# Windowed attention and a shrinking MLP on one core: the masks of the first three tiles move from TensorE to VectorE, in a new order

## The chip, the cores and the metric

The kernel runs on one core of a Trainium2 chip. The metric is the device time of one execution in microseconds (us). Each time shown is of one execution; the median of several is compared. The core has TensorE (PE, matrix products into the eight PSUM banks), VectorE (DVE), ScalarE (ACT), GpSimd (POOL) and SyncE (SP). POOL, SP and ACT issue DMAs, each into a queue of its own.

## The reference, cut to what matters

```python
scores = scale * np.matmul(q, k.transpose(0, 1, 3, 2))       # 4 batches, 8 heads, 768 positions, head size 64
keep = is_global | is_local                                   # first 8 keys, or the last 96 before the query
bias = -slopes[:, None, None] * dist[None, :, :]              # one slope a head, dist 96 for far global keys
a = softmax(np.where(keep, scores + bias, -1e9))
x = (a @ v).transpose(0, 2, 1, 3).reshape(3072, 512)
h = x @ w_in                                                  # 512 x 2048
out = (h - np.tanh(h)) @ w_out                                # 2048 x 512
```

The inputs and the output are float32; the kernel multiplies in bfloat16 and sums in float32.

## The kernel before, in words

The 3072 rows are 24 tiles (u = 0 to 23) of 128 queries. Tiles 0 to 3 are the first of each batch and have one block of keys, their own. All others have two: their own and the previous tile's, into whose buffer the batch's first 8 (global) keys and values are copied (K.u, V.u). All heads of a tile are worked on together.

The whole program is one list written out by hand, ORDER (lines 17 to 65). Each word is an action, and every engine runs its own words in the order in which they stand there, one behind the other; semaphores are set by what the actions read and write. HOMES (lines 66 to 104) says which buffer or PSUM bank each value lives in, so that an action also waits until the former holder has been read. The words, with the lines that the profile shows:

- lq.u, lk.u, lv.u load queries, keys, values. For u < 3 (HW, line 141) q and k come in float32 over ACT's and SP's queue (L294) and are cast into kq by cq.u, ck.u (a suffix /a is ScalarE, /d VectorE; L229 and L231). All other loads go over POOL's queue, which casts on the way (L294 for u of 3 and 4, L297 from there on). in.j (L300) and out.j (L303) load the weights, also on POOL.
- rel (POOL, L235) writes the distances; from it VectorE makes dist (L240 to L242), slopes (L265), first (L245 to L249), turn and ident, and writes the ones beside the values (ones, L271). zero is a tile of zeros. table is an action that issues no instruction; ScalarE's table load is shown with em's line (L280).
- T.u turns q and k: on TensorE for u < 7 (PE_T; L317, L321, L312), followed by two evictions Te.u.1 (keys) and Te.u.0 (queries); by a DMA transpose on SP's queue from u = 7 on (L333).
- bm.m (TensorE, L275) multiplies dist by the slopes, two 128x512 products, and em.m (ScalarE, L280) takes exp of that: mk.m, a multiplicative mask. There are three: 0 for the first tile of a batch, 1 for the own block, 2 for the previous block.
- S.n are the scores of one or several blocks (L352). E.u.o is exp of a block (ScalarE, L359), M.u.o its product with the mask (VectorE, L363). AV.u multiplies by the values (L378), R.u divides (VectorE, L386 and L387), X.u transposes the result (L398), Xe.u evicts it into xT; from u = 8 on a DMA transpose does both.
- m1.g.f is x @ w_in for a group of tiles (L420), th its tanh (ScalarE, L430), g the difference (VectorE, L436), m2.u.c.a one of four parts of the second product (L445), ev its eviction and st the store (L454).

The first three tiles (BIASED = 3, line 144) differ: B.u (lines 343 to 345) puts dist times slopes into the PSUM bank first and S.u adds the scores to it, so that exp gives the masked weights at once and there is no M.u.

```python
def a_B(u):
    for o in blocks(u):
        bias(("s", u, o), mask_of(u, o), False)
```

The first actions of each queue, as ORDER has them: SP lk.1 lk.0 lk.2; ACT lq.1 lq.0 lq.2 table em.1 em.0 cq.0; POOL rel lq.3 lk.3 lv.0 lq.4 lk.4 lv.1 lv.2 in.1 in.0 lv.3 in.2; VectorE zero ones.0 slopes dist turn first ident ones.1 cq.1 ck.1 ck.0 Te.1.0 Te.0.0 ck.2 Te.3.0 Te.2.0 R.0 R.1 M.3.0; TensorE bm.1 bm.0 B.1 T.1 B.0 T.0 S.1 T.3 B.2 S.0 T.2 S.3 AV.0 S.2 AV.1 X.0 T.4 X.1 AV.2 bm.2 m1.0.0 AV.3 X.2 m1.1.0 X.3 S.4.

Of the kernel before, what the change touches and what calls it, by code (L numbers as in the profile page):

```python
# [22 lines left out]
lq.6 m1.1.4 th.2.0 M.4.1 m1.2.2 th.1.4 g.2.0 m1.0.4 th.2.6 g.1.4 lv.5 th.2.2 T.5 g.2.6 m1.1.8 th.0.4 Te.5.0/d Te.5.1/a
g.0.4 m1.0.8 th.1.8 g.2.2 lq.10 S.5 th.0.8 g.1.8 m1.2.10 E.5.1 g.0.8 m1.2.8 K.5 th.2.10 M.5.1 m2.2.0.0 lv.6 E.5.0
g.2.10 m1.2.4 th.2.8 M.5.0 m2.1.0.0 g.2.8 th.2.4 m2.0.0.0 g.2.4 out.3 m2.2.0.1 lk.8 m2.2.0.2 m2.0.0.1 AV.4 lq.7
m1.1.12 V.4 lk.10 R.4 m1.2.14 th.1.12 lq.8 m1.0.12 g.1.12 th.2.14 lk.9 g.2.14 m1.2.12 th.0.12 lk.7 m2.1.0.1 g.0.12
th.2.12 lq.9 X.4 g.2.12 AV.5 Xe.4/a m2.1.0.2 R.5 T.6 V.5 lv.7 m2.0.0.2 Te.6.1/a Te.6.0/d lk.11 X.5 m2.2.0.3 Xe.5/a
m2.0.0.3 ev.2.0/a T.10 S.6 ev.0.0/a m1.3.10 T.8 E.6.1 K.6 m1.3.0 E.6.0 M.6.1 T.7 m1.3.2 th.3.10 M.6.0 m2.3.0.0 T.9
th.3.2 g.3.10 m1.3.4 th.3.0 g.3.2 m2.1.0.3 g.3.0 th.3.4 AV.6 g.3.4 ev.1.0/a m1.3.6 R.6 st.1.0 m1.3.12 lv.15 th.3.6 V.6
m2.3.0.1 g.3.6 lq.12 th.3.12 S.7 g.3.12 lv.8 m2.3.0.2 E.7.1 K.7 lv.17 m1.3.8 E.7.0 lk.13 M.7.1 X.6 m2.3.0.3 Xe.6/d  # L30
lv.10 th.3.8 M.7.0 S.8 ev.3.0/a st.0.0 g.3.8 AV.7 lv.9 E.8.1 m1.3.14 V.7 R.7 lq.11 E.8.0 m2.4.0.0 M.8.1 lq.18 X.7
th.3.14 m2.4.0.1 M.8.0 lk.12 Xe.7/a S.9 g.3.14 lq.13 AV.8 E.9.1 K.9 m2.4.0.2 lq.15 R.8 E.9.0 m1.4.6 lv.11 M.9.1 Xe.8
m2.4.0.3 M.9.0 th.4.6 lv.12 T.11 m1.4.8 g.4.6 ev.4.0/a S.10 T.12 th.4.8 AV.9 E.10.1 K.10 g.4.8 m1.4.0 T.13 R.9 E.10.0
m2.5.0.0 M.10.1 Xe.9 m1.4.4 th.4.0 V.9 M.10.0 m1.4.10 th.4.4 g.4.0 m2.5.0.1 th.4.10 g.4.4 AV.10 lq.14 g.4.10 m2.5.0.2
R.10 lv.16 m1.4.2 V.10 lv.13 Xe.10 S.11 th.4.2 lk.15 m2.5.0.3 g.4.2 E.11.0 lk.14 K.11 m1.4.12 K.12 ev.5.0/d E.11.1
st.4.0 m1.4.14 M.11.0 lk.17 th.4.12 M.11.1 m2.6.0.0 th.4.14 st.5.0 g.4.12 m2.6.0.1 E.12.0 g.4.14 AV.11 M.12.0 m2.7.0.0
R.11 m2.7.0.1 V.11 Xe.11 S.12 m2.7.0.2 T.15 E.12.1 m2.7.0.3 E.13.1 M.12.1 T.14 m2.6.0.2 ev.7.0/d E.13.0 AV.12 M.13.1
st.7.0 m2.6.0.3 lq.16 M.13.0 m1.5.7 R.12 ev.6.0/a lv.14 m1.5.6 th.5.7 V.12 Xe.12 lk.16 m1.5.1 g.5.7 th.5.6 lq.17 AV.13
g.5.6 th.5.1 lv.18 m1.5.3 R.13 lq.23 m1.5.0 th.5.3 g.5.1 Xe.13 lk.18 m1.5.11 g.5.3 th.5.0 m1.5.8 g.5.0 lq.19 th.5.11
S.13 g.5.11 lk.19 th.5.8 m1.5.4 g.5.8 E.14.0 T.16 K.14 m1.5.2 K.15 E.14.1 M.14.0 T.17 m1.5.9 th.5.4 M.14.1 m1.5.13  # L40
th.5.2 g.5.4 m1.5.14 E.15.0 g.5.2 m1.5.10 th.5.13 M.15.0 th.5.14 m1.5.5 g.5.13 T.18 th.5.10 g.5.14 m2.8.0.0 th.5.5
g.5.10 m1.5.15 th.5.9 g.5.5 AV.14 th.5.15 g.5.9 m2.8.0.1 T.19 V.14 R.14 m1.5.12 m2.8.0.2 g.5.15 Xe.14 th.5.12 S.14
g.5.12 m2.9.0.0 E.15.1 K.16 m2.8.0.3 E.16.0 M.15.1 m2.9.0.1 ev.8.0/d E.16.1 AV.15 M.16.0 st.8.0 m2.10.0.0 lv.19 R.15
m2.9.0.2 lk.23 V.15 Xe.15 M.16.1 S.15 lv.22 m2.9.0.3 E.17.1 K.17 lv.23 m2.10.0.1 ev.9.0/d E.18.0 st.6.0 m2.10.0.2
M.17.1 lq.22 E.17.0 M.18.0 m2.10.0.3 st.3.0 st.2.0 M.17.0 AV.16 lv.21 m2.11.0.0 V.16 T.23 R.16 lv.20 AV.17 m2.11.0.1
R.17 st.9.0 Xe.16 ev.10.0/a m2.11.0.2 lk.20 V.17 Xe.17 m1.6.0 st.10.0 lq.21 S.16 th.6.0 lq.20 m2.11.0.3 g.6.0 E.19.1
K.19 lk.21 m1.6.9 ev.11.0/d E.19.0 m1.6.6 M.19.1 th.6.9 M.19.0 m1.6.4 th.6.6 g.6.9 m1.6.3 E.18.1 lk.22 g.6.6 m1.6.15
th.6.4 M.18.1 th.6.3 AV.19 g.6.4 AV.18 th.6.15 g.6.3 m1.6.12 R.18 m1.6.2 th.6.12 V.19 Xe.18 m1.6.8 g.6.15 th.6.2 R.19
m1.6.7 th.6.8 g.6.12 Xe.19 m1.6.1 th.6.7 g.6.8 m1.6.11 th.6.1 T.20 g.6.7 m1.6.5 th.6.11 g.6.1 T.21 m1.6.10 g.6.11
th.6.5 g.6.2 m1.6.14 th.6.10 T.22 g.6.5 m1.7.12 th.6.14 g.6.10 m1.6.13 th.7.12 g.6.14 m1.7.1 g.7.12 th.6.13 m1.7.10  # L50
g.6.13 th.7.1 S.17 g.7.1 th.7.10 m2.13.0.0 g.7.10 E.21.0 K.21 m2.12.0.0 K.20 E.20.0 M.21.0 m2.13.0.1 E.20.1 M.20.0
m2.12.0.1 M.20.1 m2.13.0.2 AV.20 m1.7.14 V.20 R.20 m2.13.0.3 th.7.14 Xe.20 m1.7.9 g.7.14 ev.13.0/a m2.12.0.2 th.7.9
m2.12.0.3 g.7.9 S.18 ev.12.0/a m1.7.5 E.21.1 K.22 m2.14.0.0 E.22.0 M.21.1 m1.7.3 th.7.5 M.22.0 m1.7.2 th.7.3 g.7.5
m2.14.0.1 E.22.1 g.7.3 AV.21 th.7.2 M.22.1 m2.14.0.2 V.21 g.7.2 m2.14.0.3 R.21 m1.7.0 ev.14.0/a Xe.21 S.19 st.14.0
th.7.0 m1.7.13 E.23.0 g.7.0 AV.22 th.7.13 M.23.0 m2.19.0.0 E.23.1 R.22 m1.7.7 V.22 Xe.22 m1.7.4 M.23.1 th.7.7 g.7.13
m2.18.0.0 th.7.4 g.7.7 m2.17.0.0 g.7.4 AV.23 m1.7.6 R.23 m1.7.8 th.7.6 Xe.23 m1.7.11 g.7.6 th.7.8 m2.18.0.1 g.7.8
th.7.11 m2.19.0.1 g.7.11 m2.19.0.2 m2.15.0.0 m2.16.0.0 m1.7.15 m1.8.0 th.7.15 m2.15.0.1 g.7.15 th.8.0 m1.8.1 g.8.0
m2.19.0.3 th.8.1 m1.8.15 g.8.1 ev.19.0/a m1.8.6 st.19.0 th.8.15 st.12.0 m1.8.3 g.8.15 th.8.6 m1.8.9 g.8.6 th.8.3
m2.17.0.1 g.8.3 th.8.9 m1.8.7 g.8.9 m1.8.10 th.8.7 m1.8.4 g.8.7 th.8.10 m2.15.0.2 g.8.10 th.8.4 m1.8.2 g.8.4 m1.8.5
th.8.2 m2.15.0.3 g.8.2 th.8.5 m1.8.11 g.8.5 ev.15.0/a m2.16.0.1 th.8.11 m2.20.0.0 g.8.11 m2.17.0.2 m2.22.0.0 m2.17.0.3  # L60
m1.8.8 ev.17.0/a m2.22.0.1 st.17.0 th.8.8 st.11.0 m2.21.0.0 g.8.8 m2.22.0.2 m2.18.0.2 m2.18.0.3 m1.8.13 ev.18.0/a
m2.20.0.1 st.18.0 th.8.13 m2.16.0.2 g.8.13 m2.16.0.3 m1.8.14 ev.16.0/a m1.8.12 th.8.14 m2.21.0.1 g.8.14 th.8.12
# [4 lines left out]
mk.0:2,3 mk.1:0,1 mk.2:6,7 f32.0.k:3 kq.0:1 f32.0.q:2 f32.1.k:1 kq.1:0 f32.1.q:0 f32.2.k:5 kq.2:3 f32.2.q:4 v.0:0
v.1:1 kq.3:2 v.2:2 kq.4:4 v.3:3 v.4:4 kq.5:0 v.5:5 kq.6:1 v.6:6 kq.7:4 v.7:7 kq.8:3 v.8:9 kq.9:0 v.9:4 kq.10:2 v.10:11
kq.11:1 v.11:5 kq.12:2 v.12:6 kq.13:3 v.13:7 kq.14:1 v.14:9 kq.15:0 v.15:8 kq.16:3 v.16:0 kq.17:2 v.17:10 kq.18:4
v.18:4 kq.19:1 v.19:11 kq.20:2 v.20:7 kq.21:4 v.21:6 kq.22:3 v.22:5 kq.23:0 v.23:1 tr.0.0:1 tr.0.1:7 qk.0:1 s.0.0:2,3  # L70
p.0.0:1 av.0:2,3 x.0:0 xt.0:2 xT.0:0 tr.1.0:6 tr.1.1:0 qk.1:0 s.1.0:4,5 p.1.0:0 av.1:4,5 x.1:1 xt.1:1 xT.1:1 tr.2.0:4
# [517 lines left out]
```

## Time and profile before

| What | us |
|---|---|
| median of three runs | 215.25 |
| the three runs | 214.08, 216.29, 215.25 |
| the profiled execution | 215.35 |
| its span, from the first instruction to the last | 213.5 |
| TensorE busy | 204.6 |
| VectorE busy | 130.4 |
| ScalarE busy | 120.5 |
| POOL busy | 76.9 |

A line of the timeline or of a group names the engine, the line, the operation, the tile written and the tiles read, the shape, and how often (x); times are us from the start of the span. Where two rows of the timeline overlap on one engine, the engine has begun the next instruction before the last has drained, so the step from start to start is shorter than the duration. The chain of waits follows the program back from its last instruction, at each step to what released it. Busy times by stretch have, behind the stretch and its length, the busy time and the number of instructions of each engine, the granted clock of TensorE, the mean load of the DMA engines and GB/s.

### The profile page before, as it was taken

How to read it: one execution, taken by the hardware profiler on the slowest of the kernel's cores; microseconds unless marked ns; L12 is line 12 of the kernel's file. 1: busy time of each engine (PE TensorE's matmuls, PEld its weight loads, DVE VectorE, ACT ScalarE, POOL GpSimd, SP SyncE). 2: the span in 40 equal slices, each digit the busy share in tenths (PEclk: the TensorE clock that was granted, in tenths of full speed). 3: DMA queues.
4: the chain of work that ended last, by engine and by line, in shares of the span. 5: the costliest groups of instructions: out<-in, count | busy, mean ns of one | idle time of the engine just before them, and what ended most of it. 6: DMA issues, size and time to landing. Idle time of an engine off the chain costs nothing.

```text
span 213.5 us, 4492 instructions
## 1 busy us (share of the span) xinstructions
PE 204.6 (96%) x1796; PEld 117.2 (55%) x1796; DVE 130.4 (61%) x264; ACT 120.5 (56%) x179; POOL 76.9 (36%) x101
## 2 busy tenths in 40 slices
...
GB/s 164 243 177 189 208 198 175 179 157 194 128 177 150 141 154 216 181 151 137 175 53 166 195 206 150 147 3 25 0 78 25 25 3 98 0 0 98 52 116 228
DMA packets 100884, 27.55 MB, mean 129 GB/s; under 512 B 91840, under 2 KB 99264, under 8 KB 100864
## 3 DMA queue, kind: packets, MB, share of 16 engines
...
q1 hardware_dynamic: 28048, 8.13, 23.5%
...
## 4 chain that ended last, share of the span: by engine, by line
PE 68%; issue 12%; DMA 10%; POOL 6%; DVE 1%; ACT 0%; SPq 0%; POOLq 0%; DVEq 0%; ACTq 0%
PE ps L420 30%; PE ps L445 28%; DMA qk<-kq 4%; POOL kq L297 3%; PE ps L352 3%; DMA f<-in_k_dram 3%; PE ps L378 3%; DMA out_dram<-ot 3%; POOL vb L297 2%; PE ps L398 1%; PE ps L317 1%; POOL out_dram L454 1%; PE ps L321 1%; PE ps L275 1%; PE ps L312 0%
## 5 line engine op out<-in xcount | busy, mean ns | idle before, releaser
L445 PE MATMUL ps<-w_out_bf,g 128*128 128x512 bf16 (+2 forms) x400 | 91.2, 371 | 0.0
L420 PE MATMUL ps<-xT,w_in_bf 128*128 128x512 bf16 (+2 forms) x576 | 90.5, 308 | 0.5 <-ACT ot L229 0.5
L436 DVE TENSOR_TENSOR g<-ps,th 128x512 bf16<-128x512 f32 x96 | 65.0, 688 | 38.7 <-ACT th L430 37.5
L430 ACT ACTIVATE th<-ps 128x512 f32<-128x512 f32 x96 | 56.7, 599 | 45.6 <-PE ps L420 44.8
L420 PEld LDWEIGHTS <-w_in_bf 128*128 128x128 bf16 x576 | 50.2, 98 | 33.9 <-issue 0.8
L445 PEld LDWEIGHTS <-g 128*128 128x128 bf16 x400 | 37.0, 98 | 38.0 <-DVE g L436 0.5
L454 POOL DMA_DIRECT2D out_dram<-ot x21 | 12.0, 576 | 106.3 <-ACT ot L229 86.5
L359 ACT ACTIVATE pr<-ps 128x1024 bf16<-128x1024 f32 x44 | 43.0, 1023 | 9.8 <-PE ps L352 9.8
L363 DVE TENSOR_TENSOR pr<-pr,mk 128x1024 bf16<-128x1024 bf16 x41 | 27.6, 687 | 8.0 <-ACT pr L359 7.9
L229 ACT COPY ot<-ps 128x512 f32<-128x512 f32 (+2 forms) x20 | 11.3, 565 | 26.6 <-PE ps L445 19.2
L297 POOL DMA_DIRECT2D vb<-in_v_dram x24 | 21.7, 912 | 5.1 <-DMA w_out_bf<-in_moe_w_out_dram 2.6
L297 POOL DMA_DIRECT2D kq<-in_q_dram x19 | 17.1, 911 | 12.4 <-DMA qk<-kq 8.2
L297 POOL DMA_DIRECT2D kq<-in_k_dram x19 | 17.1, 903 | 1.2 <-PE ps L352 0.5
L387 DVE TENSOR_TENSOR x<-ps,rden 128x512 bf16<-128x512 f32 x24 | 16.6, 692 | 0.8
L378 PEld LDWEIGHTS <-pr 128*128 128x128 bf16 x352 | 13.5, 98 | 4.2 <-issue 0.2
L378 PE MATMUL ps<-vb,pr 128*128 128x65 bf16 x352 | 14.8, 194 | 0.0
L352 PEld LDWEIGHTS <-qk 64*128 64x128 bf16 x352 | 10.2, 96 | 7.0 <-issue 6.3
L352 PE MATMUL ps<-qk 64*128 64x128 bf16 x192 | 10.1, 229 | 0.0
L231 DVE COPY vb<-vb 8x512 bf16<-8x512 bf16 x16 | 5.7, 356 | 5.9 <-PE ps L378 5.9
L275 PE MATMUL ps<-slopes,dist 128*128 128x512 bf16 x12 | 5.4, 587 | 3.1 <-DVE dist L242 3.1
L352 PE MATMUL ps<-qk,qk 64*128 64x128 bf16 x160 | 7.8, 217 | 0.0
L386 DVE RECIPROCAL rden<-ps 128x8 f32<-128x8 f32 x24 | 4.8, 199 | 2.8 <-PE ps L378 2.6
...
## 6 DMA issues: line engine op xcount, KB each, us to landing
...
w_out_bf<-in_moe_w_out_dram POOLq DMA_DIRECT2D x4, 512.0 KB, 13.1
w_in_bf<-in_moe_w_in_dram POOLq DMA_DIRECT2D x3, 512.0 KB, 10.5
...
```

Of the source, the lines that this page charges most:

```text
L229: nc.scalar.copy(out=out, in_=in_)
L297: eng(e).dma_start(out=dst, in_=rows_of(src, u).rearrange("h p d -> p h d"))
L352: nc.tensor.matmul(bank(("s", u, o), hh)[:, p * P : (p + 1) * P], buf(("qk", back[u] if o else u))[r, 1, p, :], buf(("qk", u))[r, 0, p, :] ...
L359: nc.scalar.activation(d, banks(("s", u, o), 0, 1), AF.Exp, bias=0.0, scale=scale)
L363: nc.vector.tensor_tensor(out=t, in0=t, in1=mk[:, mask_of(u, o)], op=ALU.mult)
L378: nc.tensor.matmul(t[:, h // (H // 2), h % (H // 2), :], buf(("p", u, o))[:, slot(h), :], buf(("v", back[u] if o else u))[:, h, 0 : Dh + 1 ...
L387: nc.vector.tensor_tensor(out=buf(("x", u)).rearrange("q (a h) d -> q a h d", a=2), in0=t[:, :, :, 0:Dh], in1=rden.to_broadcast([P, 2, H / ...
L420: nc.tensor.matmul(t[:, (f - f0) * n : (f - f0 + 1) * n], w_in_bf[j][:, c, fo : fo + P], x[:, c, 0:n], start=(c == 0), stop=(c == CD - 1),)
L430: nc.scalar.activation(h_view(buf(("th", g, f0)), g, m), h_view(bank(("h", g, f0)), g, m), AF.Tanh, bias=0.0, scale=1.0)
L436: nc.vector.tensor_tensor(out=buf(("g", g))[:, f0 : f0 + m, 0:n], in0=h_view(bank(("h", g, f0)), g, m), in1=h_view(buf(("th", g, f0)), g, ...
L445: nc.tensor.matmul(bank(part)[:, 0 : c1 - c0], buf(("g", g))[:, f, t * P : (t + 1) * P], w_out_bf[f // FJ][:, f % FJ, c0:c1], start=(f == ...
L454: eng(e).dma_start(out=out[turn_of[u] * P : (turn_of[u] + 1) * P, c0:c1], in_=buf(("ot", u))[:, c0:c1])
```

## The change

BIASED goes from 3 to 0: B.0, B.1 and B.2 are gone, the scores of tiles 0 to 2 start their banks themselves, and M.0.0, M.1.0 and M.2.0 multiply the masks in. warm() takes a bank, and the word zero:7 puts one product of the zero tile with itself (128x512, result unused) into bank 7. ORDER and HOMES are written anew throughout; all other actions are the same. The core of the diff, with the start of both orders and the stretch of the new one that holds lv.12 to T.11's loads:

```diff
 ORDER = """
-lq.1 lk.1 zero rel ones.0 lq.0 lk.0 lq.3 slopes lq.2 lk.2 lk.3 dist table lv.0 turn bm.1 first ident lq.4 ones.1 bm.0
-em.1 lk.4 cq.1/d ck.1/d B.1 lv.1 em.0 T.1 lv.2 B.0 cq.0/a ck.0/d in.1 Te.1.0/d Te.1.1/a T.0 in.0 S.1 Te.0.1/a Te.0.0/d
-cq.2/a ck.2/d E.1.0 lv.3 T.3 B.2 in.2 Te.3.1/a Te.3.0/d S.0 lk.5 T.2 E.0.0 lq.5 S.3 Te.2.0/d Te.2.1/a AV.0 in.3 R.0
-E.3.0 S.2 AV.1 out.0 X.0 R.1 E.2.0 T.4 out.1 M.3.0 X.1 Xe.0/a AV.2 bm.2 Te.4.1/d Xe.1/a out.2 m1.0.0 R.2 Te.4.0/a em.2
...
+lq.1 lk.1 zero lk.3 ones.0 zero:7 lq.0 lk.0 zero:7 rel zero:7 dist table lk.2 zero:7 slopes zero:7 lq.2 turn bm.1
+first ident ones.1 bm.0 em.1 lv.1 cq.1/d zero:7 ck.1/d lq.3 em.0 T.1 lv.0 cq.0/d ck.0/a zero:7 Te.1.1/d in.1 Te.1.0/a
+T.0 cq.2/a ck.2/d lv.2 S.1 Te.0.1/d Te.0.0/a T.2 in.0 E.1.0 S.0 Te.2.0/d lv.3 Te.2.1/d E.0.0 in.2 M.1.0 lq.4 M.0.0
+AV.1 T.3 lk.4 R.1 S.2 Te.3.1/a AV.0 in.4 E.2.0 Te.3.0/d in.3 R.0 S.3 lq.5 E.3.0 M.2.0 X.0 X.1 lk.5 Xe.0/d AV.2 Xe.1/a
+bm.2 M.3.0 m1.0.0 lv.4 em.2 R.2 AV.3 m1.1.0 th.0.0 R.3 X.2 lv.5 th.1.0 g.0.0 X.3 m1.1.4 Xe.2/a Xe.3/d out.0 g.1.0
+m1.2.6 th.1.4 out.1 g.1.4 m1.2.2 th.2.6 T.4 g.2.6 th.2.2 m1.2.0 Te.4.1/d Te.4.0/a lq.6 m1.2.4 g.2.2 th.2.0 m1.0.4
...
+ev.3.0/a AV.7 E.8.1 m1.3.12 lv.12 V.7 R.7 E.8.0 m2.4.0.1 st.1.0 M.8.1 lq.11 X.7 th.3.12 S.9 M.8.0 Xe.7/a lk.11
...
-    BIASED = 3
+    BIASED = 0
...
-    def warm():
-        nc.tensor.matmul(ps[:, 7, :], zero[:, 0, :], zero.to_broadcast([P, 4, P]), start=True, stop=True)
+    def warm(b):
+        nc.tensor.matmul(ps[:, b, :], zero[:, 0, :], zero.to_broadcast([P, 4, P]), start=True, stop=True)
...
-            if word == "warm":
-                warm()
+            if word.startswith("zero:"):
+                warm(int(word[5:]))
```

By queue, the new start reads: SP lk.1 lk.0 lk.2 as before; ACT lq.1 lq.0 table lq.2 em.1 em.0 ck.0 Te.1.0 cq.2 Te.0.0 E.1.0 E.0.0 Te.3.1 E.2.0 E.3.0; POOL lk.3 rel lv.1 lq.3 lv.0 in.1 lv.2 in.0 lv.3 in.2 lq.4 lk.4 in.4 in.3 lq.5 lk.5 lv.4 lv.5 out.0; VectorE zero ones.0 dist slopes turn first ident ones.1 cq.1 ck.1 cq.0 Te.1.1 ck.2 Te.0.1 Te.2.0 Te.2.1 M.1.0 M.0.0 R.1 Te.3.0 R.0 M.2.0 Xe.0 M.3.0 R.2 R.3; TensorE five zeros, bm.1 bm.0, a zero, T.1, a zero, T.0 S.1 T.2 S.0 AV.1 T.3 S.2 AV.0 S.3 X.0 X.1 AV.2 bm.2 m1.0.0 AV.3 m1.1.0 X.2 X.3 m1.1.4 m1.2.6 m1.2.2 T.4.

More of the change, by code (lines that the diff above doesn't have):

```diff
@@ L23 @@
[L23 to L62, printed above, removed]
@@ new lines @@
+AV.1 T.3 lk.4 R.1 S.2 Te.3.1/a AV.0 in.4 E.2.0 Te.3.0/d in.3 R.0 S.3 lq.5 E.3.0 M.2.0 X.0 X.1 lk.5 Xe.0/d AV.2 Xe.1/a
+bm.2 M.3.0 m1.0.0 lv.4 em.2 R.2 AV.3 m1.1.0 th.0.0 R.3 X.2 lv.5 th.1.0 g.0.0 X.3 m1.1.4 Xe.2/a Xe.3/d out.0 g.1.0
+m1.2.6 th.1.4 out.1 g.1.4 m1.2.2 th.2.6 T.4 g.2.6 th.2.2 m1.2.0 Te.4.1/d Te.4.0/a lq.6 m1.2.4 g.2.2 th.2.0 m1.0.4
+g.2.0 th.2.4 g.2.4 S.4 th.0.4 lk.6 m1.0.8 E.4.1 K.4 g.0.4 out.2 m1.0.12 th.0.8 M.4.1 lv.6 m1.2.14 E.4.0 g.0.8 out.3
+T.5 th.0.12 M.4.0 m1.1.8 lk.8 Te.5.0/a g.0.12 m1.2.8 th.2.14 Te.5.1/d th.1.8 g.2.14 m1.2.10 th.2.8 g.1.8 lv.15 S.5
@@ new lines @@
+th.2.10 g.2.8 m1.1.12 E.5.0 g.2.10 m2.1.0.0 K.5 E.5.1 M.5.0 m2.0.0.0 lq.7 th.1.12 M.5.1 AV.4 lk.7 g.1.12 m2.2.0.0 lv.8
+R.4 m2.2.0.1 V.4 X.4 m2.0.0.1 Xe.4/a m1.2.12 lq.8 AV.5 lq.12 th.2.12 m2.1.0.1 V.5 g.2.12 T.6 R.5 m2.0.0.2 Te.6.0/a
+Te.6.1/d m2.2.0.2 lk.10 S.6 lq.9 X.5 E.6.0 K.6 m2.1.0.2 lk.9 Xe.5/d m2.3.0.0 lv.7 E.6.1 M.6.0 T.7 m1.3.10 lq.10 M.6.1
+m2.0.0.3 lv.9 th.3.10 T.8 m1.3.6 g.3.10 ev.0.0/a lv.13 m1.3.0 th.3.6 lv.17 m1.3.8 g.3.6 th.3.0 m2.3.0.1 g.3.0 th.3.8
+AV.6 g.3.8 m1.3.14 T.9 lv.11 V.6 R.6 m1.3.2 th.3.14 m2.3.0.2 g.3.14 th.3.2 m2.1.0.3 g.3.2 lq.13 S.7 T.10 lk.12
@@ new lines @@
+m1.5.4 th.5.2 M.15.0 lk.18 m1.5.7 th.5.10 g.5.2 lv.16 E.14.1 T.16 m1.5.6 g.5.10 th.5.7 m1.5.1 M.14.1 T.17 th.5.6 g.5.7
+m1.5.13 th.5.1 g.5.6 m1.5.14 th.5.4 g.5.1 th.5.13 m1.5.9 g.5.4 th.5.14 m2.8.0.0 g.5.13 th.5.9 g.5.14 AV.14 T.18
+m2.8.0.1 g.5.9 lq.21 V.14 AV.13 R.14 lv.19 m1.5.12 R.13 Xe.14 m2.8.0.2 lk.21 th.5.12 S.14 g.5.12 Xe.13 m2.9.0.0 E.15.1
+K.16 m2.8.0.3 E.16.0 M.15.1 m2.9.0.1 ev.8.0/d E.16.1 AV.15 M.16.0 st.8.0 m2.10.0.0 lv.22 V.15 R.15 m2.9.0.2 lv.23
+M.16.1 Xe.15 S.15 m2.10.0.1 E.17.1 K.17 T.21 m2.10.0.2 E.17.0 M.17.1 AV.16 m2.10.0.3 E.18.0 M.17.0 V.16 m2.9.0.3
@@ new lines @@
+ev.10.0/a R.16 AV.17 st.10.0 ev.9.0/a M.18.0 Xe.16 m2.11.0.0 lq.20 R.17 m2.11.0.1 lq.22 V.17 Xe.17 S.16 st.9.0 lk.20
+m1.6.5 E.18.1 K.19 m2.11.0.2 E.19.0 M.18.1 m1.6.1 th.6.5 M.19.0 m1.6.8 th.6.1 g.6.5 AV.18 E.19.1 g.6.1 m1.6.6 R.18
+th.6.8 m1.6.3 th.6.6 M.19.1 Xe.18 m1.6.13 th.6.3 g.6.8 m1.6.2 T.20 th.6.13 g.6.6 AV.19 g.6.13 th.6.2 m1.6.4 R.19
+m1.6.0 th.6.4 g.6.2 Xe.19 m1.6.10 V.19 th.6.0 g.6.3 m1.6.9 th.6.10 g.6.4 m1.6.14 g.6.10 th.6.9 g.6.0 m2.11.0.3 th.6.14
+g.6.9 m1.6.12 ev.11.0/a g.6.14 m1.7.11 st.11.0 th.6.12 lk.22 m1.6.11 g.6.12 th.7.11 lv.20 m1.6.15 g.7.11 th.6.11
```

101 lines of the change are left out of this document (61 added, 40 removed).

## The prediction

> **What bounds the kernel now.** I read the page first (busy shares), then TensorE's waits, the busy time by stretch, the chain of waits, and last the timeline of the first 21 us. From the page:
>
> ```profile
> span 213.5 us, 4492 instructions
> PE 204.6 (96%) x1796; PEld 117.2 (55%) x1796; DVE 130.4 (61%) x264; ACT 120.5 (56%) x179; POOL 76.9 (36%) x101
> ```
>
> TensorE (PE) is busy 96%. Where the other 4% lies, the waits from 16.7 us on and the busy time by stretch tell (columns: length, then PE, PEld, DVE, ACT, POOL busy):
>
> ```profile
> PE ps L420 <- ACT ot L229: 0.5, 1, 0.5
> ...
> 0.00:9.00 9.00, 4.48 (x17) 1.84 (x18) 4.35 (x33) 4.21 (x5) 7.69 (x14) 1.00 0.86 207
> 9.00:16.60 7.60, 6.87 (x83) 4.61 (x83) 4.07 (x8) 5.62 (x8) 5.91 (x8) 1.00 1.84 180
> 16.60:120.00 103.40, 103.11 (x1110) 66.93 (x1111) 75.46 (x145) 64.95 (x95) 53.72 (x65) 1.00 1.67 167
> 120.00:210.40 90.40, 90.17 (x588) 43.84 (x587) 46.48 (x80) 45.49 (x73) 9.55 (x16) 1.00 0.44 73
> ```
>
> From 16.6 to 210.4 us PE is busy 193.28 of 193.80 us, and the same products stand in the new order. Nothing is to be won there; only the first 17 us can shorten, and any stall comes on top. The chain of waits in the start:
>
> ```profile
> 1.54 6.92 DMA f<-in_k_dram
> ...
> 8.49 0.44 DVE kq L231
> ...
> 8.97 1.05 PE ps L317 x8
> ...
> 10.12 0.70 DVE qk L231
> ...
> 10.87 1.06 PE ps L321 x16
> 11.93 0.97 PE ps L275 x2
> 12.89 0.54 PE ps L352 x8
> 13.44 0.96 PE ps L317 x8
> 14.40 0.54 PE ps L352 x8
> 14.94 0.57 PE ps L378 x8
> ```
>
> lk.0 lands at 8.46; then TensorE works almost without a gap, and slowly: the timeline has equal groups S.0 and S.2 (8 matmuls) at two speeds, 2.6 us apart, and X.3 as the last of the start:
>
> ```profile
> 12.83 0.61 PE L352 MATMUL ps<-qk 64*128 64x128 bf16 x8
> ...
> 15.43 0.40 PE L352 MATMUL ps<-qk 64*128 64x128 bf16 x8
> ...
> 20.80 0.40 PE L398 MATMUL ps<-ident,x 128*128 128x128 bf16 x4
> ```
>
> The step from one group to the next falls from 0.54 us to about 0.3 at 15.4 us. So TensorE ran at half speed until then, though the granted clock beside the stretches reads 1.00 from the start: that column does not show this state, the durations do.
>
> **The change part by part.** Base: the profiled run, 215.35 us (span 213.5 and 1.85 around it), 0.1 above the median of 215.25 and within 214.08 to 216.29.
>
> Bias products. B.1 and B.0 end at 7.55, before lk.0 lands: removing them is worth nothing, the load covers them. B.2 is 0.97 us of the chain (line above).
>
> Masks. M.0.0, M.1.0, M.2.0 add 3 x 0.68 us on VectorE (M.3.0's row, L363). Each also puts a wait between exp and AV: M.1.0 waits for E.1.0, with M.0.0, R.1, Te.3.0 and R.0 queued behind it; S.3 and X.0 wait for those.
>
> VectorE also takes Te.2.1 and Xe.0 from ScalarE (0.69, 0.42) and gives it Te.1.0 and Te.0.0. Its idle time from 8.9 to 21.2 is 4.5 us now (0.61, 0.71, 1.78, 0.40, 0.39, 0.49 before its instructions); the new work uses nearly all of it.
>
> Constants. lk.3 goes ahead of rel on POOL, and POOL's first transfer takes 1.03 us, so rel ends near 2.3, not 1.18, and dist and slopes 1.1 us later: bm.1 starts near 4.3, not 3.11. Its cover is lk.0: cq.1, ck.1, cq.0 (0.43 each) end near 6.5 and T.1 by 7.3. Without that cover it would cost the 1.1.
>
> Seven zero products. 0.46 us each as bm's (2.74 us for six): 3.2 us, all in idle time (1.0 to 3.1; 6.0 to 6.4; 7.3 to 7.7). Hidden by rel and lk.0. They may keep TensorE at full speed for T.0; that is the forecast, and its failure a rival.
>
> Early loads. SP's three are unmoved. On ACT's queue the word table now stands ahead of lq.2, but it issues nothing: the table load (2.81, 1.28 us) has em.1's line, L280, and should stay behind lq.2, so I take nothing. If it does come first, lq.2 lands by 10.1 + 1.28 (it had landed when cq.2 ran at 10.10), cq.2 ends at 12.0 and T.2, which ck.2 holds until 10.6, follows: the upper end, +1.3. POOL's first transfer starts at 0.84, not 1.38, and takes a share of the DMA 0.54 us earlier: lk.0 and lk.2 land 0 to 0.54 later. I take half, +0.25. lq.4 and lk.4 go behind in.2: issued near 9 and 10, plus 7.5 (median of such loads) to 10.5 (of the w_in's), they land by 20.5, and T.4 comes at 22.5: hidden. in.4 moves forward, out.0 behind lv.5: out.0's first user, m2.1.0.0, comes at 33.5, its issue at 15 plus 13.1 is 28: hidden.
>
> The new start. lk.2 lands by 10.1 (issued 2.4, longest landing 7.7). In VectorE's new queue ck.2 stands ahead of Te.0.1, so from there VectorE runs through: ck.2 0.5, then Te.0.1, Te.2.0, Te.2.1, M.1.0, M.0.0 (starts 0.61 apart, as 17.29 and 17.89 now), to 13.6; R.1 0.85, Te.3.0 0.61, R.0 0.85, M.2.0 ends 16.6. At full speed TensorE follows: AV.1 13.15, T.3 until 14.05, S.2, AV.0, S.3 at 15.2 (waits for Te.3.0), X.0 at 16.05. ScalarE's E.1.0, E.0.0, E.2.0, E.3.0 end 11.6, 12.8, 15.5, 16.7, ahead of their masks. Then AV.2 16.65 (0.24), bm.2 (0.43), m1.0.0 (0.89), AV.3 ends 18.6, R.3 18.7 to 19.6, X.3 at 19.65. Now X.3 starts at 20.80 with T.4 (0.57) already behind it; the new order has T.4 later. Gain: 20.80 - 0.57 - 19.65 = 0.58. With the later loads 0.58 - 0.25 = 0.33: 215.35 - 0.33 = 215.0. Range of this case alone: 214.3 (nothing later, and the two waits of 0.4 and 0.5 gone in part) to 216.6 (lq.2's 1.3 and the loads' other 0.29 added).
>
> Tail. Both orders end with the two parts of m2.23, two stores on SP after them, and POOL's last stores 3.5 us or more ahead: no change.
>
> **The rivals.**
>
> Half speed lasts (slower). The five early zeros end at 3.1 but bm.1 waits until 4.3, and after T.1 the PE idles from 7.7 to 9.2. The row to go by: now it works from 3.11 to 7.55 almost without a gap and from 8.97, with one gap of 0.32, and it is fast only at 15.4, 4.6 us after the last gap. If the new start too stays slow: T.0 and T.2 0.5 longer, T.3, S.2, AV.0 0.9 together, so R.0 starts at 16.45, M.2.0 ends at 18.0, X.3 near 21.2, 1.5 later than above, against the B.2 and VectorE time already counted: 0.6 slower than now. Full speed 4.6 us after 13.7 (AV.1 to S.3 without a gap) costs little more: 215.35 + 0.6 + 0.25 = 216.2. If the gap ahead of X.0 starts the count anew, it lasts until about 22: half of the 4 us of dense work from 18 is lost, 218.0. Point: 217.0. It decides if the S groups still step 0.54 us at 16 us. For it: the gaps, wider than now. Against: 7 more products.
> [...]
>
> TensorE stalls on a load (slower). In the middle T.11 lands at 74.56 (chain: 7.73 us of DMA from 66.83) and S.11, which reads it, starts at 75.41: 0.85 us to spare. In the new POOL queue lq.11 and lk.11 stand behind lv.12 and st.1.0; lv.12's buffer comes free with AV.7, near 59.9, so lk.11 is issued near 62.3, lands 3 to 7.5 later, and its transpose takes 4.5 to 7.7: between 69.8 and 77.5, against S.11 near 74.8. Price 0 to 2.7, so 215.0 to 217.7; point 216.5. It decides from a landing of lk.11 after 67. For it: the thin margin now; against: POOL is idle before lv.12, so its queue is short.
>
> VectorE's row of work starts earlier (faster). By 10.1 the DMAs have moved six f32 loads (256 KB each) and two of POOL's. If POOL's quarter gave way, lk.2 would land a quarter of some 8 us, 2.0, earlier: 213.0. Against it: POOL issues its first load earlier than now, not later.
>
> **How the numbers follow.** Forecast 0.58 (215.0), half speed 0.24 (217.0), stall 0.10 (216.5), earlier loads 0.08 (213.0). About 1% (2.15 us, below 213.1 or above 217.4) is what a measurement tells from no change. Faster: 0.08 and 0.03 of the forecast's edge, 0.11. Slower: half of the two slower rivals, 0.17. Same: 0.72. The range from 213.3 to 217.4 leaves out most of the last rival and the upper halves of the first two, 2 in 10.
>
> **What would show it.** Right: VectorE without a gap from ck.2 to R.0; S.0 and S.2 both stepping near 0.3 us; X.3 at 19.6 to 20; PE dense after. Wrong: S.2 still at 0.61; T.1 after 8; a PE wait at S.11; lk.2 landing away from 10 to 10.6. The forecast fails as a whole if PE has over 1 us of gaps after 20 us.

## The result, and the profile after

| What | before | after |
|---|---|---|
| median of 20 runs, us | 214.88 | 216.89 |
| shortest and longest run, us | 212.77, 217.77 | 215.19, 218.48 |
| the profiled execution, us | 215.35 | 216.21 |
| its span, us | 213.5 | 214.3 |
| its mean granted clock | 1.00 | 0.984 |

The ratio after to before is 1.0103, with a 95% interval from 1.0082 to 1.0124: about 2.2 us slower, just over the 1% that can be told from no change, and inside the range. The ratio and the counts of runs below leave out runs that were over 1.5% above the fastest of the same kernel. The two profiled executions are only 0.86 us apart: the one of before was longer than 13 of its 20 runs, the one of after is the fifth shortest of its 20. The trace of after therefore shows less than half of the loss.

The page of after:

```profile
span 214.3 us, 4509 instructions
...
PE 206.2 (96%) x1797; PEld 118.5 (55%) x1797; DVE 132.4 (62%) x268; ACT 121.2 (57%) x178; POOL 76.6 (36%) x101
```

TensorE is busy 1.6 us longer, with three bias products of 128x1024 fewer and seven zero products more. The waits of TensorE in after (us in all, how many, the longest), then its busy time by stretch:

```profile
PE ps L379 <- DVE pr L364: 1.7, 1, 1.7
...
PE ps L399 <- DVE x L388: 0.5, 1, 0.5
PE ps L353 <- DMA qk<-kq: 0.4, 1, 0.4
```

```profile
0.00:9.00 9.00, 6.72 (x27) 2.82 (x27) 5.44 (x34) 4.70 (x6) 7.84 (x14) 1.00 0.94 210
9.00:16.60 7.60, 5.39 (x86) 4.00 (x85) 6.76 (x13) 5.39 (x7) 5.33 (x8) 0.78 1.73 185
16.60:120.00 103.40, 103.40 (x1113) 67.57 (x1112) 73.55 (x143) 65.08 (x94) 52.00 (x64) 0.98 1.68 168
120.00:211.00 91.00, 90.62 (x586) 44.08 (x578) 46.70 (x80) 45.76 (x71) 11.44 (x18) 1.00 0.44 73
```

From 16.6 us on TensorE is as dense as before; the only wait there is 0.4 us for a DMA transpose (S.18, at 146.5). The loss that this trace shows lies between 9 and 20 us, where the column of the granted clock (the third from the end) falls to 0.78. The timeline of TensorE there:

```profile
9.21 0.61 PE L353 MATMUL ps<-qk 64*128 64x128 bf16 x8
...
10.36 0.40 PE L353 MATMUL ps<-qk 64*128 64x128 bf16 x8
12.48 0.42 PE L379 MATMUL ps<-vb,pr 128*128 128x65 bf16 x8 [1.73 <-DVE pr L364]
...
13.43 0.61 PE L353 MATMUL ps<-qk 64*128 64x128 bf16 x8
...
15.62 1.03 PE L399 MATMUL ps<-ident,x 128*128 128x128 bf16 x8 [0.48 <-DVE x L388]
...
17.74 1.91 PE L421 MATMUL ps<-xT,w_in_bf 128*128 128x128 bf16 x16
...
20.91 0.61 PE L399 MATMUL ps<-ident,x 128*128 128x128 bf16 x8
```

S.1 runs at half speed (0.61), S.0 at full speed (0.40). Then AV.1 waits 1.73 us for M.1.0, and S.2 is at 0.61 again. m1.0.0, 16 matmuls, takes 1.91 us; the same group took 1.06 before. X.3, in the last group shown, starts at 21.13. The same stretch cut into pieces of 3.4 us shows the clock itself:

```profile
9.90:13.30 3.40, 1.67 (x40) 1.35 (x38) 2.85 (x7) 1.93 (x4) 2.68 (x4) 1.00 1.80 182
13.30:16.70 3.40, 2.92 (x44) 2.25 (x40) 3.11 (x7) 2.63 (x4) 2.57 (x4) 0.50 1.57 194
16.70:20.10 3.40, 3.40 (x37) 2.84 (x34) 1.39 (x3) 2.01 (x3) 1.17 (x3) 0.50 1.33 202
20.10:30.00 9.90, 9.90 (x155) 9.03 (x154) 8.16 (x15) 7.27 (x13) 6.51 (x8) 1.00 1.65 189
```

Full speed came near 9.9 us, was lost again at 13.3 after a piece in which TensorE was busy for 1.67 of 3.40 us, and came back at 20.1, after the first piece without a gap. Two pieces of 3.4 us at half are 3.4 of 214.3 us lost, which is the mean clock of 0.984. Of after's 19 remaining runs, 13 show that mean or less, with a median of 217.01 us. Two show 0.992, what one such piece at half would take from the mean (1.7 of 214.3 us), with 215.19 and 216.00 us, and four show 0.998 or more, with 215.38 to 216.75 us. So by their mean clock most runs lose two pieces but not all, and the runs without any loss are still slower than before's median.

The balance of the two profiled executions: X.3 starts 0.33 us later than before and T.4's 0.57 is still to come, so the start is 0.90 longer; the waits behind it are 0.38 against 0.48. That makes 0.80, against 0.86 between the two times.

### The profile page after: what moved, and what is told of

Same layout as the page of the kernel before. It is cut to its first block, busy times and chain, and to the rows that moved or that the text cites. A ratio compares the mean times of both kernels' runs of the same rounds, so it can differ in the third digit from the quotient of the medians.

```text
span 214.3 us, 4509 instructions
## 1 busy us (share of the span) xinstructions
PE 206.2 (96%) x1797; PEld 118.5 (55%) x1797; DVE 132.4 (62%) x268; ACT 121.2 (57%) x178; POOL 76.6 (36%) x101
## 4 chain that ended last, share of the span: by engine, by line
PE 88%; DMA 5%; DVE 3%; issue 1%; POOL 1%; ACT 0%; POOLq 0%; DVEq 0%
PE ps L446 37%; PE ps L421 36%; PE ps L379 5%; PE ps L353 5%; DMA qk<-kq 4%; DMA kq<-in_k_dram 2%; PE ps L318 1%; PE ps L399 1%; DVE qk L232 1%; PE ps L322 1%; DVE kq L232 0%; PE ps L313 0%; ACT ot L230 0%; DVE slopes L266 0%; POOL kq L295 0%
## 5 line engine op out<-in xcount | busy, mean ns | idle before, releaser
L421 PEld LDWEIGHTS <-w_in_bf 128*128 128x128 bf16 x576 | 51.0, 99 | 33.5 <-issue 0.6
L364 DVE TENSOR_TENSOR pr<-pr,mk 128x1024 bf16<-128x1024 bf16 x44 | 29.9, 688 | 8.2 <-ACT pr L360 7.8
L230 ACT COPY ot<-ps 128x512 f32<-128x512 f32 (+2 forms) x21 | 11.9, 565 | 23.1 <-PE ps L446 19.9
L379 PEld LDWEIGHTS <-pr 128*128 128x128 bf16 x352 | 14.3, 100 | 6.2 <-DVE pr L364 1.9
L388 DVE TENSOR_TENSOR x<-ps,rden 128x512 bf16<-128x512 f32 x24 | 16.6, 692 | 0.8
L379 PE MATMUL ps<-vb,pr 128*128 128x65 bf16 x352 | 15.3, 197 | 1.7 <-DVE pr L364 1.7
L232 DVE COPY qk<-qk 128x32 bf16<-128x32 bf16 x16 | 3.7, 287 | 6.0 <-PE ps L353 5.9
L232 DVE COPY vb<-vb 8x512 bf16<-8x512 bf16 x16 | 4.4, 278 | 4.5 <-PE ps L379 4.5
```

Of the source, the lines that this page charges most:

```text
L230: nc.scalar.copy(out=out, in_=in_)
L364: nc.vector.tensor_tensor(out=t, in0=t, in1=mk[:, mask_of(u, o)], op=ALU.mult)
L379: nc.tensor.matmul(t[:, h // (H // 2), h % (H // 2), :], buf(("p", u, o))[:, slot(h), :], buf(("v", back[u] if o else u))[:, h, 0 : Dh + 1 ...
L388: nc.vector.tensor_tensor(out=buf(("x", u)).rearrange("q (a h) d -> q a h d", a=2), in0=t[:, :, :, 0:Dh], in1=rden.to_broadcast([P, 2, H / ...
L421: nc.tensor.matmul(t[:, (f - f0) * n : (f - f0 + 1) * n], w_in_bf[j][:, c, fo : fo + P], x[:, c, 0:n], start=(c == 0), stop=(c == CD - 1),)
```

## The experiments

All ratios are to runs of the kernel before on the same chip in the same comparison, with 95% intervals. L-numbers of kernels that keep the new program are those of after; the old program with zeros in its start has them too.

**Fill the gap.** The first theory was that the wait for M.1.0 costs the clock and the clock costs the time. Seven zero products were put into the gap:

```diff
-T.2 in.0 E.1.0 S.0 Te.2.0/d
+T.2 in.0 E.1.0 S.0 zero:7 zero:7 zero:7 zero:7 zero:7 zero:7 zero:7 Te.2.0/d
```

> The changed kernel with seven more products of the zero tile (128x512, unused) between S.0 and AV.1, where its TensorE waited 1.73 us for M.1.0. Clock theory: that wait costs TensorE its full speed at 13.3 us for 6.8 us (0.98 granted from 16.6 on), which the dense work of the start pays; with the wait filled, S.2 and X.0 stay at full speed (0.40 us each instead of 0.61), X.3 starts near 19.4 instead of 21.1, and the time falls by 1.5 to 2 us, to the kernel before or up to 0.5 us below it. Rival, VectorE theory: the three masks lengthen VectorE's row of work whatever TensorE's speed; X.3 stays near 21 and the time 1% above the kernel before.

Measured: 1.0062 (1.0033 to 1.0091); 11 of 12 runs have a clock of 0.998 or more. By stretch, and by TensorE's longest wait, in this kernel:

```profile
9.90:13.30 3.40, 3.34 (x48) 1.86 (x47) 3.18 (x7) 2.02 (x4) 2.49 (x4) 1.00 1.81 181
13.30:16.70 3.40, 2.58 (x48) 1.89 (x47) 3.37 (x8) 3.03 (x5) 2.57 (x4) 1.00 1.59 197
```

```profile
PE ps L421 <- DMA xT<-x: 1.3, 1, 1.3
```

The gap does cost the clock: the same piece of time, now busy for 3.34 us, is followed by full speed, even though the next one holds more idle time than in after. From AV.1 to the start of the X.2 and X.3 group it is 6.20 us instead of 8.43, so X.3 starts 2.3 us earlier. But the time falls by only some 0.9 us (1.0103 to 1.0062; the two intervals overlap a little, so it may be anything from 0.1 to 1.6 us). Of the rest the trace shows one piece in the middle: m1.5.3 waits 1.3 us for Xe.11, whose transpose lands at 87.75, and S.11 starts at 75.01 as T.11 lands. The profiled execution is the second shortest of the twelve, so what the others lose beyond that is not seen. Half of the theory stands.

**The masks and the zeros, one at a time.** Are the three new products on VectorE what costs? In the new order the bias products were put back, and the three products taken out:

```diff
-    BIASED = 0
+    BIASED = 3
...
-T.0 cq.2/a ck.2/d lv.2 S.1 Te.0.1/d Te.0.0/a T.2 in.0 E.1.0 S.0
+T.0 cq.2/a ck.2/d lv.2 B.1 S.1 Te.0.1/d Te.0.0/a T.2 in.0 E.1.0 B.0 S.0
...
-T.3 lk.4 R.1 S.2
+T.3 lk.4 R.1 B.2 S.2
```

> The changed kernel with BIASED back at 3: B.1, B.0, B.2 stand just ahead of S.1, S.0, S.2 and the three masks on VectorE are gone; the new order and the seven zero products stay. Clock theory: AV.1 then waits for exp alone, TensorE's gap ahead of it falls from 1.73 to 0.3 us or less, half speed does not come back, X.3 starts between 19 and 19.8 and the time is 0.3 to 1.5 us below the kernel before. VectorE theory: the same direction, with 1.8 us (three starts 0.61 apart) less on VectorE. A third, order theory (the new order itself is slower, the masks are not to blame): the time stays 1% above the kernel before.

Measured: 1.0135 (1.0090 to 1.0179). Its trace has full speed in time and X.3 at 18.93, and then loses the time again in the middle:

```profile
PE ps L421 <- DMA xT<-x: 1.3, 1, 1.3
...
PE ps L353 <- DMA qk<-kq: 0.8, 2, 0.5
```

So in the new order the masks are not what costs: without them, and with the clock kept in the trace, the kernel is no faster.

After without its seven zero products:

```diff
-lq.1 lk.1 zero lk.3 ones.0 zero:7 lq.0 lk.0 zero:7 rel zero:7 dist table lk.2 zero:7 slopes zero:7 lq.2 turn bm.1
+lq.1 lk.1 zero lk.3 ones.0 lq.0 lk.0 rel dist table lk.2 slopes lq.2 turn bm.1
...
```

> The changed kernel without its seven zero products, all else the same. Clock theory: T.0, T.2 and S.0 run at half speed as well (0.61 for S.0 instead of 0.40), TensorE then reaches AV.1 at the same time, since M.1.0 sets it, and full speed comes only with the dense work, near 18 to 21 us: the time is 0 to 1 us above the changed kernel. VectorE theory: the zeros bring nothing, the time is that of the changed kernel within 0.3 us.

Measured: 1.0133 (1.0090 to 1.0177), with the same 1.7 us for M.1.0. The zeros are not what costs, and six runs can't show what they bring.

The other way round, the kernel before with the masks on VectorE and nothing else changed:

```diff
-    BIASED = 3
+    BIASED = 0
...
-in.2 Te.3.1/a Te.3.0/d S.0 lk.5 T.2 E.0.0 lq.5
+in.2 Te.3.1/a Te.3.0/d M.1.0 S.0 lk.5 T.2 E.0.0 M.0.0 lq.5
...
-E.2.0 T.4 out.1 M.3.0
+E.2.0 T.4 out.1 M.2.0 M.3.0
```

> The kernel before with the masks of the first three tiles on VectorE (BIASED = 0; M.1.0 behind Te.3.0, M.0.0 behind exp of tile 0, M.2.0 ahead of M.3.0; B.0 to B.2 gone), in its own order and without zeros. Clock theory: TensorE's row in the old order has T.2 and S.3 ahead of AV.0, so the wait for M.0.0 stays under 1 us, half speed ends near 15 to 17 us as before, and the time is within 0.7 us of the kernel before. VectorE theory: three masks of 0.61 lengthen the start by 1 to 1.8 us: the time is 0.5 to 0.9% above the kernel before.

Measured: 0.9991 (0.9958 to 1.0024). TensorE's waits for the masked weights in this kernel:

```profile
PE ps L378 <- DVE pr L363: 0.5, 2, 0.3
```

Two waits of 0.3 us at most, paid for by the bias products that are gone. In the old order the masks cost nothing that can be measured either: the theory that VectorE's new work is the cost falls. What is left is the order.

**The queue in the middle.** In after, POOL has 5.13 us of idle time in front of lv.12, whose buffer becomes free with AV.7. (The row names V.7, a copy on VectorE. But V.7 stands behind lv.12 in ORDER and itself waits for AV.7, which ends at 62.13.) Behind it stand st.1.0, lq.11 and lk.11 (timeline of POOL in after: start, time, then the idle time before it in brackets):

```profile
56.44 0.88 POOL L298 DMA_DIRECT2D kq<-in_k_dram  x1 [0.33 <-issue]
62.44 0.87 POOL L298 DMA_DIRECT2D vb<-in_v_dram  x1 [5.13 <-DVE vb L232]
63.31 0.57 POOL L455 DMA_DIRECT2D out_dram<-ot  x1
63.87 0.89 POOL L298 DMA_DIRECT2D kq<-in_q_dram  x1
64.75 1.76 POOL L298 DMA_DIRECT2D kq<-in_k_dram  x2
```

T.11, which turns what lk.11 loads, is issued at 71.3 and lands at 76.7; S.11 starts at 77.23. The next kernel moves the loads ahead of the blocked one:

```diff
-M.7.1 lk.16 th.3.4
+M.7.1 lk.16 lq.11 lk.11 th.3.4
...
-st.1.0 M.8.1 lq.11 X.7 th.3.12 S.9 M.8.0 Xe.7/a lk.11 m2.4.0.2
+st.1.0 M.8.1 X.7 th.3.12 S.9 M.8.0 Xe.7/a m2.4.0.2
...
-S.10 st.3.0 ev.4.0/a
+S.10 st.3.0 lk.15 lq.15 ev.4.0/a
...
-M.10.0 T.11 m1.4.4
+M.10.0 T.11 lq.14 lk.14 m1.4.4
...
```

> The changed kernel with four pairs of loads moved in POOL's queue: lq.11 and lk.11 ahead of lv.12 and st.1.0 (which wait for AV.7), and lk.15, lq.15, lq.14, lk.14 ahead of st.5.0 (which waits for the eviction of tile 5). Clock theory alone: nothing in the middle costs time as long as the start is 2 us late, so the time stays within 0.3 us of the changed kernel, 1.0% above the kernel before. Middle theory (from the profile of the kernel with the gap filled: TensorE waits 1.3 us at m1.5.3 for the transpose Xe.11, and S.11 runs the moment T.11 lands): stalls there, which differ from run to run, are most of the loss, and the time falls by 0.8 to 1.5 us.

> Both edits: the gap ahead of AV.1 filled with seven zero products and the loads of tiles 11, 14 and 15 moved forward. Both theories together: the start is 2 us earlier and nothing in the middle takes it back: no wait of TensorE over 0.6 us behind 20 us, and the time is 0.5 to 1.5 us below the kernel before (ratio 0.993 to 0.998). If the ratio stays near the 1.006 of the filled gap alone, the loads are not what takes the gain back.

Measured: 1.0116 (1.0082 to 1.0149) for the moved loads alone, 1.0071 (1.0046 to 1.0096) with the gap filled as well. The first stays within 0.3 us of after, as the clock theory had it, and misses the middle theory. The second misses the 0.993 to 0.998 that both theories together gave; it stays near the filled gap alone. The timeline of TensorE in the first of the two shows one reason:

```profile
66.83 0.41 PE L379 MATMUL ps<-vb,pr 128*128 128x65 bf16 x8
68.70 0.40 PE L379 MATMUL ps<-vb,pr 128*128 128x65 bf16 x8 [1.47 <-ACT ot L230]
```

AV.8 takes one of the banks that ev.4.0 on ScalarE has to empty, and waits 1.47 us for it. That eviction writes the buffer from which st.1.0 is being stored, until 68.0, and E.10 stands behind it on ScalarE. With the gap filled as well the same wait is 0.8 us. The store was as much behind lv.12 as the loads were, so one late transfer had taken the other's place. The third version has the gap filled, the loads moved, and st.1.0 moved too:

```diff
-ev.1.0/a m2.2.0.3 E.7.1
+ev.1.0/a st.1.0 m2.2.0.3 E.7.1
...
-E.8.0 m2.4.0.1 st.1.0 M.8.1
+E.8.0 m2.4.0.1 M.8.1
```

> The changed kernel with the gap filled and lq.11, lk.11, lk.15, lq.15, lq.14, lk.14 moved forward, and st.1.0 ahead of lk.16 as well, which now waits behind lv.12 and so kept ev.4.0 (same output buffer) and the exps behind it on ScalarE: TensorE waited 0.8 to 1.5 us at AV.8. Theory that POOL's queue order in the middle is what is left of the loss: that wait goes, no other over 0.5 us takes its place, and the ratio falls from 1.007 to 1.003 or less. Rival: the wait moves to the next user of the DMA engines (S.11, m1.5.3 or S.18), the ratio stays within 0.002 of 1.007.

Measured: 1.0011 (0.9974 to 1.0049). The timeline of POOL in this kernel, with the store now at 55.48, and TensorE's waits for DMAs:

```profile
55.48 0.58 POOL L455 DMA_DIRECT2D out_dram<-ot  x1
...
59.35 0.87 POOL L298 DMA_DIRECT2D kq<-in_q_dram  x1 [2.15 <-DMA qk<-kq]
60.22 0.88 POOL L298 DMA_DIRECT2D kq<-in_k_dram  x1
61.08 0.89 POOL L298 DMA_DIRECT2D vb<-in_v_dram  x1
```

```profile
PE ps L353 <- DMA qk<-kq: 1.0, 1, 1.0
...
PE ps L421 <- DMA xT<-x: 0.4, 1, 0.4
```

lk.11 is issued near 60 instead of near 65, the wait at AV.8 is gone, and the kernel can't be told from the one before. Waits of 1.0 us (S.11) and 0.4 us (m1.5.3) for transposes remain, in a start that is earlier than before's. Against after, the filled gap and the moved transfers together bring back 2.0 us (1.0103 to 1.0011), clear of the noise. The step from the filled gap alone (1.0062) is one of medians only, and by the two intervals it may be anything from almost nothing to 1%. No trace shows how it comes about: the two profiled executions (215.03 with the gap filled, 215.09 here) don't differ, and T.11 is issued at 68.0 and lands at 75.8 here, against 68.4 and 75.0 with the gap filled alone; lk.11 took 7.6 us to land and T.11 7.8.

**The same wait, with and without the loss.** The kernel with the moved loads alone has the wait for M.1.0 too, and its trace keeps full speed:

```profile
11.81 0.42 PE L379 MATMUL ps<-vb,pr 128*128 128x65 bf16 x8 [1.68 <-DVE pr L364]
...
12.72 0.40 PE L353 MATMUL ps<-qk 64*128 64x128 bf16 x8
```

In after the record of the granted clock begins at 9.90 us, with full speed, and changes at 13.31 and 20.14: the stretches between are 3.41 and 6.83 us long, once and twice 3.41. In before its one stretch at full speed goes from 15.42 to 213.39, 58 times 3.413. So the clock seems to change only at edges 3.41 us apart in these two. In this kernel the record of the clock begins at 7.57 us; with the same spacing the next edge is at 10.98, and the wait, from 10.13 to 11.81, lies across it. In the kernel without zeros, cut at the change at 14.25, it lies within one piece. The pieces of the two:

```profile
7.57:10.98 3.41, 2.41 (x38) 1.53 (x35) 2.83 (x5) 3.41 (x6) 3.21 (x4) 1.00 1.89 184
10.98:14.40 3.42, 2.06 (x48) 1.61 (x48) 3.35 (x8) 2.04 (x4) 2.37 (x3) 1.00 1.88 177
```

```profile
10.83:14.25 3.42, 1.69 (x42) 1.27 (x42) 3.20 (x6) 1.68 (x3) 2.33 (x5) 1.00 1.82 180
14.25:17.66 3.41, 2.99 (x36) 2.38 (x35) 3.25 (x8) 2.71 (x4) 2.53 (x3) 0.50 1.42 199
17.66:21.07 3.41, 3.41 (x63) 3.20 (x62) 2.57 (x6) 2.53 (x4) 1.80 (x3) 1.00 1.30 205
```

Without zeros half speed lasts one piece, in after two. So in these three traces the same wait cost nothing, 3.4 us or 6.8 us at half speed, and where the edges fall goes with it. Full speed was lost after the pieces that were busy for 1.67 us (after) and 1.69 us (without zeros) and kept after those of 2.41 and 2.06 us (loads moved). Four pieces don't show a rule.

**Is it the DMAs, and is it the new order's DMAs?** The filled kernel and the kernel before were both run with light loads of v, one head of eight once a buffer has been filled; the other seven heads are left out, so these kernels do not compute the reference:

```diff
+    filled = set()
+
+    def load_v(e, u):
+        hs = 1 if home(("v", u))[0] in filled else H
+        filled.add(home(("v", u))[0])
...
-        op(("lv", u), POOL, lambda e, u=u: load_natural(e, buf(("v", u))[:, :, 0:Dh], v, u))
+        op(("lv", u), POOL, lambda e, u=u: load_v(e, u))
```

> The changed kernel with the gap ahead of AV.1 filled, and the second and later loads into each buffer of values cut from eight heads to one (12 of the 24 loads; the tiles' other seven heads keep an earlier tile's values, so the output differs). Nothing else moves less data. Middle theory (transposes and loads of the middle are late because they share the DMA engines with POOL's loads): TensorE has no wait over 0.3 us behind 20 us, and the time falls by 1 us or more against the filled gap alone, to the kernel before or below it. Rival (the middle is not the cause, the loss lies in the start): the time stays near 1.006 of the kernel before.

> The same cut of loads in the kernel before (12 of the 24 loads of values with one head; the output differs). Middle theory: the old order had next to no waits in the middle, so the time stays within 0.4 us of the kernel before. If it falls as much as in the new order, the lighter loads help any order, and the comparison says nothing of the new one.

Measured: 0.9966 (0.9932 to 1.0001) in the filled new order, 0.9961 (0.9925 to 0.9998) in the old one. The new order wins some 2.1 us by it (from 1.0062), the old one 0.8. With light loads no wait of TensorE for a DMA is left behind 20 us in the filled kernel, and the two orders are equal. This points to transfers that come late as what the new order has to pay apart from the clock. The old order pays some of that too, more than I had expected: the difference between the two gains, 1.2 us, is no larger than its own uncertainty.

**Two questions on the start.** Does lv.0 ahead of lk.3 in POOL's first loads set when lk.0 lands? And would zeros in the old start bring something?

```diff
-lq.2 lk.2 lk.3 dist table lv.0 turn bm.1
+lq.2 lk.2 lv.0 dist table lk.3 turn bm.1
```

> The kernel before with lv.0 ahead of lk.3 in POOL's queue, nothing else changed: a load of values (four times as many, smaller packets) second, as in the changed kernel, where lk.0 landed at 7.17 us instead of 8.46. Theory that the small-packet load leaves the queues of SP and ACT more of the DMA engines: lk.0 lands between 7.1 and 7.7 and lk.2 by 9.2. Rival, that lk.0 came earlier because lk.3 was issued before rel or because of the run: lk.0 stays at 8.2 to 8.8. T.3 then waits for lk.3, which lands up to 0.9 later, so the time changes by less than 0.7 us either way.

```diff
-lq.1 lk.1 zero rel ones.0 lq.0 lk.0
+lq.1 lk.1 zero rel ones.0 warm warm warm warm warm lq.0 lk.0
...
-T.1 lv.2 B.0 cq.0/a
+T.1 lv.2 B.0 warm warm warm cq.0/a
```

> The kernel before with eight zero products: five ahead of bm.1, three between B.0 and T.0, where TensorE waited 1.42 us. Theory that half speed in the start is paid on the path: full speed comes by 9 to 12 us instead of 15.4, T.3, S.0, T.2 and AV.0 run in half the time, X.0 starts 0.7 to 1.5 us earlier, and the time is 0.5 to 1.3 us below the kernel before. Rival: the chain of evictions (VectorE and ScalarE) sets the start, the time is the same within 0.3 us.

The first: 1.0009 (0.9986 to 1.0033), with lk.0 at 7.56. It settles nothing, because the second, whose POOL queue is that of before, has lk.0 at 7.07 (before: 8.46; the old order with masks: 9.31). That landing differs by 2 us between executions of the same loads.

The second: 1.0012 (0.9984 to 1.0039). Full speed is there at 5.9 us and X.0 starts at 13.29 instead of 16.59. TensorE's waits in it:

```profile
PE ps L379 <- DMA vb<-in_v_dram: 0.9, 1, 0.9
...
PE ps L421 <- DMA w_in_bf<-in_moe_w_in_dram: 0.5, 1, 0.5
```

m1.0.0 now waits for in.0 and AV.3 for lv.3, so X.3 starts at 19.25. That is 1.55 us earlier than before's, of which the earlier lk.0 can account for 1.39. In the median nothing is left of it. The runs of before beside the first experiments say the same: 10 of 23 show a clock of 0.992 or less, with a median of 214.0 us, and the other 13 have 214.6. So half speed in the old start costs nothing that can be measured. That loads bound the same stretch is a reading of this one trace.

**All of the change but its order.** The kernel before with the masks on VectorE and five and five zeros in its start:

```diff
-    BIASED = 3
+    BIASED = 0
...
-lq.1 lk.1 zero rel ones.0 lq.0 lk.0
+lq.1 lk.1 zero rel ones.0 warm warm warm warm warm lq.0 lk.0
...
-B.1 lv.1 em.0 T.1 lv.2 B.0 cq.0/a
+lv.1 em.0 T.1 lv.2 warm warm warm warm warm cq.0/a
...
```

> All of the change but its order: the kernel before, masks of the first three tiles on VectorE, and ten zero products (five ahead of bm.1, five between T.1 and T.0). Order theory: neither masks nor zeros cost anything, the time is 0 to 0.8 us below the kernel before. VectorE theory: 0.5 to 0.9% above it.

Measured: 1.0002 (0.9968 to 1.0035). Without the new order there is no loss, and no gain. No kernel that computes the whole reference was faster than the one before by more than its interval.

## Why the prediction was wrong

It said no change, with 215.0; it came out 1.03% slower, at 216.89. The term that was expected to win 0.33 us lost 0.90 in the profiled start. The rival that had one chance in ten, transfers that come late, came on top; that is read from the versions, since after's own trace has only 0.4 us of such waits.

**The failed step: "At full speed TensorE follows: AV.1 13.15, T.3 until 14.05, S.2, AV.0".** The sum let TensorE wait for M.1.0 and go on at full speed. AV.1 in fact began 0.67 us earlier than that, at 12.48, and still X.3 came 1.5 us later, at 21.13 and not 19.65. From AV.1 to X.3 the sum had 6.50 us; after took 8.65, and with the gap filled, at full speed, it is 6.49. So the chain of work was right and its speed was not. The rival "half speed lasts" had asked whether full speed would come late. It came early, at 9.9, and was lost again to the wait that the change itself adds, 1.73 us in a piece that was busy for 1.67 of 3.40. The decisive sign named there, S.2 still at 0.61, is in the trace. It had a chance of 0.24, and its X.3 near 21.2 was right. Its time, 217.0, came close partly by luck: filling the gap brings back about 0.9 of 2.2 us, so the clock seems to explain less than half.

**The second failed step: "Nothing is to be won there; only the first 17 us can shorten, and any stall comes on top".** The first half holds for both profiled executions. But the stall was priced at one place, S.11, and by the thin margin of one load. lk.11 landed near 71 in after, past the 67 that was named as the rival's sign, and yet S.11 was just in time (0.5 us behind T.11), so that place alone could not decide it. The kind of loss, transfers that come late, was the right one, and it moves about: it shows at m1.5.3 when the start is earlier, at AV.8 when only the loads are moved forward, and at S.11 when the store is moved too. That their place behind lv.12 in POOL's queue is the reason rests on the medians of the three versions with the gap filled: 1.0062 and 1.0071 with the queue as it was or half mended, 1.0011 with loads and store ahead, a difference of 1.1 to 1.3 us that no trace shows at work. The expected "POOL is idle before lv.12, so its queue is short" had the sign wrong: that idle time is lv.12 blocking what stands behind it.

**The base.** The sum went from the profiled 215.35; the median over 20 runs is 214.88. From that median it would have come to 214.55, so the change was missed by 0.47 us more than 215.0 against 216.89 shows.

**What held.** bm.1 started at 4.45 (4.3 forecast). VectorE ran from ck.2 at 8.91 to the end of R.0 with two pauses of 0.52 and 0.16 us, M.2.0 ended at 16.2 (16.6 forecast), and in the old order its three products cost nothing by themselves. The word table moved no load, removing the bias products brought nothing that can be measured (0.9991 in the old order, with the masks in their place), and out.0, in.4, lq.4 and lk.4 were hidden. The tail is the same.

**Mis-sized.** lk.0 and lk.2 landed at 7.17 and 8.89 instead of 0.25 us later than before's 8.46 and 10.10. By the rival "VectorE's row of work starts earlier" this would have been a gain of over 1 us; VectorE and TensorE did start earlier, and the lost clock and the middle took it. Why those loads were earlier is open. In the eight profiled executions of the new order lk.0 lands between 6.9 and 7.6, in the six of the old one between 7.1 and 9.3, so the order may have a part in it. With lk.0 that early, the cover that the constants and the zero products were to have was gone: after's chain of waits does not run through lk.0 but through rel, the constants, T.1 and the zero product behind it.

```profile
2.22 0.39 POOL rel L236
...
8.00 0.43 PE ps L542
8.43 0.85 PE ps L318 x8
```

**What stays open.** How often each wait of the middle occurs in the runs that left no trace. Whether moving loads and store forward would do anything in after without filling the gap; only the loads alone were tried there. How the loss divides between the clock and the middle: the five versions of the new order that move all the data and kept the clock in their traces lie anywhere from 1.0011 to 1.0135. And whether the place of the edges is also what sets the runs without a trace apart.
